# A windowed attention in front of two MoE layers: row-tiled transposes of the probabilities, and an output split taken from SBUF

## The chip, the core and the metric

The program runs on one core of one Trainium2 chip. The metric is the device time of one execution in microseconds (us). The kernel before has a median of 633.68 us over three runs (633.14 to 634.17).

## What is computed

Attention with a causal window of 128 keys and 4 sink keys over 2 batches of 8 heads, 768 positions, head size 64; then two dense layers (512 to 2048 to 512) over the 1536 tokens. All inputs are float64 or float32 on the host and are worked on as pairs of a high and a low part where precision asks for it.

```python
scores = scale * np.matmul(q, k.transpose(0, 1, 3, 2))
keep = is_sink | in_window                    # 4 sinks, window of 128
scores = np.where(keep, scores, -1000000000.0)
a = np.exp(scores - np.max(scores, axis=-1, keepdims=True))
a = a / (np.sum(a, axis=-1, keepdims=True) + 1e-09)
attn = np.matmul(a, v)
x = attn.transpose(0, 2, 1, 3).reshape(B * S, H * D)
h = np.maximum(x @ w_in, 0.0);  x = h * h @ w_out        # layer 1
h = x @ w_in2;  out = (h * np.tanh(softplus(h))) @ w_out2 # layer 2
```

## The kernel before

The attention takes the first 106 us and the two layers the rest. It goes over 12 tiles of 128 queries (batch b, block i of 6), and in each over 4 pairs of heads (j). One pass of the loop `for n in range(-3, NPR + 4)` (line 541) is called a step here; two steps, an even and an odd n, are a double step, and two double steps make a tile. A step works on several pairs at once, each at another stage, and the program writes the order of each engine's work out by hand:

- `emit_s` (line 350) makes the scores of pair n+4 on TensorE: for each of the two heads three matmuls over 64 rows (L356, high and low parts), into two PSUM banks `s` out of four.
- `emit_max` (L367, DVE) masks a head's scores in PSUM and takes the extreme into `nm`; `emit_exp` (L379, ACT) takes the exponential of pair n+3 into `pr` in SBUF, with its sum. The `s` banks of a pair are free when its exponentials are done, so the scores of pair n+6 wait for them.
- On even steps `emit_rs` (L390, L391, DVE) takes the reciprocals of two pairs' sums and `emit_norm` (L399, POOL) scales those pairs' probabilities, one pair per instruction. `emit_sink` (L440, POOL) gathers the sink columns of a tile's eight heads.
- On even steps `prep` transposes a block of k or q (`tr`, L302, four 128x128 transposes) for two tiles on; ACT takes the high part (L314) and DVE the low (L320).
- Also on even steps `emit_t` (line 401) transposes the probabilities of two pairs into `pt`, one PSUM bank for each pair: per head one 128x128 block, or two from the second block of a batch on (L407, L408). `evac_t` (L415) copies one pair's bank to `pts` in SBUF in each step, on DVE for the pair j = 0 and on ACT for the other three.
- On odd steps `emit_av` (L428) multiplies `pts` with v for two pairs into the one bank `av`; its column tiles are 64 wide. Once per tile, from the third block of a batch on, the sink columns are transposed (L449, `trs`), copied (L455, DVE) and multiplied (L464).
- When a tile is complete, `emit_x` and `split_x` take its output out of PSUM: ACT casts `av` to the high part `xh` (L477) and DVE subtracts that from `av` for the low part `xl` (L483). Both read the PSUM bank `av`, which the next tile's L428 needs.

```python
401  def emit_t(b, i, j):
403      pt = ps_p.tile([P, 2, 2, P], F32, tag="pt", name="pt")
407              nc.tensor.transpose(pt[:, 0, e, :], pr[b, i][:, h, op : op + P], ident)
408          nc.tensor.transpose(pt[:, 1, e, :], pr[b, i][:, h, oc : oc + P], ident)
474  def emit_x(b, i):
477      nc.scalar.copy(hi, x)
483      nc.vector.tensor_tensor(out=lo, in0=x, in1=f32(hi), op=ALU.subtract)
```

The scores, the transposes and the products with v use TensorE in three shapes: 64 rows by 128 columns (the two heads side by side in row halves), 128 by 128, and 128 rows by 64 columns (two heads in column halves). While the attention runs, `CONV_STEPS` places the conversion of the first four weight blocks of layer 1 between the steps (L131 and L166 on POOL, L137, L141 and L147 on DVE, L162 on ACT). Its last steps have no more scores; there the first matmuls of layer 1 (L620, `h`) stand between the rest of the attention on TensorE.

Of the kernel before, what the change touches and what calls it, by code (L numbers as in the profile page):

```python
# [9 lines left out]
F32 = mybir.dt.float32  # L10
# [18 lines left out]
def kernel(  # L29
# [314 lines left out]
    def sum_at(b, i, j):  # L344
        g, s = divmod(pair_no[b, i, j] + 1, 2)
        return sums[g % len(sums)], s
# [54 lines left out]
    def emit_t(b, i, j):  # L401
        _, _, _, op, oc, _ = geom(i)
        pt = ps_p.tile([P, 2, 2, P], F32, tag="pt", name="pt")
        for e in range(2):
            h = 2 * j + e
            if op is not None:
                nc.tensor.transpose(pt[:, 0, e, :], pr[b, i][:, h, op : op + P], ident)  # L407
            nc.tensor.transpose(pt[:, 1, e, :], pr[b, i][:, h, oc : oc + P], ident)  # L408
        st["pt", b, i, j] = pt

    def evac_t(b, i, j):
        pt = st.pop(("pt", b, i, j))
        pts = apool.tile([P, 2, 2, P], F32, tag="pts", name="pts", bufs=3)
        c = slice(0 if i else 1, 2)
        (nc.vector.tensor_copy if j in EV else nc.scalar.copy)(pts[:, c], pt[:, c])  # L415
        st["pts", b, i, j] = pts
# [3 lines left out]
    def emit_av(b, i, j):  # L420
# [3 lines left out]
        pts = st.pop(("pts", b, i, j))  # L424
# [18 lines left out]
    def emit_sink_t(b, i, free):  # L443
# [4 lines left out]
        pt = free[0][:, 512 - P :] if free else ps_p.tile([P, P], F32, tag="pt", name="trs")  # L448
# [25 lines left out]
    def emit_x(b, i):  # L474
        hi, lo = x_slot(b, i)
        x = av.pop((b, i))
        nc.scalar.copy(hi, x)  # L477
        st["x"] = (x, hi, lo)
# [15 lines left out]
    with tc.manual_schedule():  # L494
# [46 lines left out]
        for n in range(-3, NPR + 4):  # L541
            at = {d: pairs[n + d] for d in range(-3, 5) if 0 <= n + d < NPR}
# [14 lines left out]
            if -3 in last:  # L557
                emit_x(*at[-3][:2])
            if 4 in at and n > -3:
                emit_max(*at[4], 0)  # L560
                emit_max(*at[4], 1)
            split_x()


            if n % 2 == 0:
                if n >= 0:
                    prep(t + 2, "kq"[j // 2])
                for d in (-1, 0):
                    if d in at:
                        emit_t(*at[d])  # L570
                if -1 in last:
# [454 lines left out]
```

## Time and profile before

| | |
|---|---|
| median of three runs | 633.68 us |
| the profiled execution, its own time | 634.14 us |
| its span (first to last instruction) | 632.4 us |
| TensorE busy (PE) | 624.2 us, 99% |
| VectorE busy (DVE) | 461.9 us, 73% |
| ScalarE busy (ACT) | 363.7 us, 58% |
| GpSimd busy (POOL) | 71.1 us, 11%, all of it in the attention |
| granted TensorE clock | full in all 40 slices of the span |

The shares of the last column are means over stages that differ: the attention uses all engines, the layers mostly TensorE. PE's busy time is that of matmuls with modelled ends that overlap; the distance between the starts of two matmuls says what one costs in a row. PEld is the loading of the stationary operand, which overlaps the matmul before it.

### The profile page before, as it was taken

To read this page: it belongs to the slowest core of one execution; us is meant where nothing else is said; L and a number is where in the kernel's file an instruction comes from. 1 tells how busy PE (TensorE), PEld (TensorE's weight loads), DVE (VectorE), ACT (ScalarE), POOL (GpSimd) and SP (SyncE) were. 2 spreads that over 40 slices of the span, in tenths; PEclk is the share of its full clock that TensorE was granted. 3 is DMA by queue.
4 is the path that set the end of the run, shared out by engine and by line. 5 is a ranking of instruction groups with operands and counts; after the bars stand their busy time and mean duration, and the time that the engine had idled before them with its cause. 6 is when DMAs were issued, how large, how long until landed. Compare 5 with 4: busy or idle time off the path is not lost.

```text
span 632.4 us, 9265 instructions
## 1 busy us (share of the span) xinstructions
PE 624.2 (99%) x3382; PEld 515.9 (82%) x3382; DVE 461.9 (73%) x968; ACT 363.7 (58%) x745; POOL 71.1 (11%) x97
## 2 busy tenths in 40 slices
PE   8999999999999999999999999999999999999996
PEld 7778787888888888888888888888888888888885
DVE  5988983999852011138889869999888888888884
ACT  5988985777744333347777745555454444544442
POOL 4686773000000000000000000000000000000000
PEclk9999999999999999999999999999999999999999
DMA  8644630666630000005666600000010000010001
GB/s 200 148 118 104 164 120 26 195 204 201 199 101 1 2 0 1 0 1 169 197 199 199 192 10 1 0 2 1 1 66 1 1 1 1 1 67 0 2 0 69
DMA packets 61189, 46.83 MB, mean 74 GB/s; under 512 B 38996, under 2 KB 55636, under 8 KB 61140
## 3 DMA queue, kind: packets, MB, share of 16 engines
q1 hardware_dynamic: 60848, 45.82, 25.0%
q8 instruction: 27, 0.44, 0.3%
q10 hardware_dynamic: 292, 0.39, 0.2%
q14 instruction: 22, 0.18, 0.1%
HBM read 43.06 MB, written 3.15 MB: 73 GB/s over the span
## 4 chain that ended last, share of the span: by engine, by line
PE 96%; DVE 2%; ACT 1%; issue 0%; DVEq 0%
PE h L620 41%; PE o L636 41%; PE s L356 4%; PE av L428 3%; PE tr L302 2%; PE pt L408 1%; PE pt L407 1%; PE idle L517 1%; PE av L464 1%; DVE s L367 1%; ACT pr L379 0%; DVE cv_a L147 0%; DVE cv_r L137 0%; ACT kh L314 0%; DVE cv_r L141 0%
## 5 line engine op out<-in xcount | busy, mean ns | idle before, releaser
L620 PE MATMUL h<-xl,wih 128*128 128x512 f32 x384 | 103.2, 390 | 0.0
L620 PE MATMUL h<-xh,wil 128*128 128x512 f32 x384 | 103.0, 390 | 0.0
L620 PE MATMUL h<-xh,wih 128*128 128x512 f32 x384 | 102.6, 389 | 0.0
L694 DVE TENSOR_TENSOR gl<-h,gh 128x512 fp32r<-128x512 f32 x48 | 33.2, 691 | 93.0 <-ACT gh L690 92.9
L620 PEld LDWEIGHTS h<-xl,wih 128*128 128x128 f32 x384 | 72.0, 188 | 15.2 <-issue 0.3
L620 PEld LDWEIGHTS h<-xh,wih 128*128 128x128 f32 x384 | 72.1, 188 | 15.0
L620 PEld LDWEIGHTS h<-xh,wil 128*128 128x128 f32 x384 | 71.9, 188 | 15.0 <-issue 0.2
L710 ACT ACTIVATE e<-t,small 128x512 f32<-128x512 f32 x48 | 34.8, 726 | 70.1 <-DVE t L706 70.1
L636 PE MATMUL o<-gh,wol 128*128 128x512 f32 x192 | 74.7, 389 | 0.0
L636 PE MATMUL o<-gl,woh 128*128 128x512 f32 x192 | 74.7, 389 | 0.0
L636 PE MATMUL o<-gh,woh 128*128 128x512 f32 x192 | 74.7, 389 | 0.0
L688 ACT ACTIVATE h<-h 128x512 f32<-128x512 f32 x48 | 27.9, 582 | 77.5 <-PE h L620 77.4
L636 PE MATMUL o<-wol,gh 128*128 128x512 f32 x176 | 68.5, 389 | 0.0
L636 PE MATMUL o<-woh,gl 128*128 128x512 f32 x176 | 68.5, 389 | 0.0
L636 PE MATMUL o<-woh,gh 128*128 128x512 f32 x176 | 68.5, 389 | 0.0
L726 ACT CAST gh<-t 128x512 fp32r<-128x512 f32 x44 | 27.4, 623 | 46.6 <-PE o L636 42.9
L399 POOL TENSOR_TENSOR pr<-pr,rs 128x544 f32<-128x544 f32 (+2 forms) x48 | 48.4, 1022 | 23.4 <-DVE rs L391 13.3
L147 DVE SCALAR_TENSOR_TENSOR cv_a<-cv_a,cv_r 128x512 int32<-128x512 int32 x64 | 44.4, 694 | 6.1
L379 ACT ACTIVATE pr<-s,nm 128x272 f32<-128x272 f32 (+2 forms) x96 | 44.4, 476 | 5.0 <-DVE nm L367 2.6
L731 DVE TENSOR_TENSOR gl<-t,gh 128x512 fp32r<-128x512 f32 x44 | 30.3, 690 | 19.8 <-ACT gh L726 19.8
L636 PEld LDWEIGHTS o<-gh,wol 128*128 128x128 f32 x192 | 36.1, 188 | 7.5
L636 PEld LDWEIGHTS o<-gl,woh 128*128 128x128 f32 x192 | 36.0, 188 | 7.5
(121 smaller groups left out, 1101.2 us busy)
## 6 DMA issues: line engine op xcount, KB each, us to landing
raw<-in_moe_w_in_dram SPq DMA_DIRECT2D x32, 512.0 KB, 3.8
raw<-in_moe_w_out_dram SPq DMA_DIRECT2D x32, 512.0 KB, 4.0
vn<-in_v_dram SPq DMA_DIRECT2D x12, 256.0 KB, 3.0
kn<-in_k_dram SPq DMA_DIRECT2D x11, 256.0 KB, 3.7
qn<-in_q_dram SPq DMA_DIRECT2D x10, 256.0 KB, 4.1
out_dram<-ob SPq DMA_DIRECT2D x8, 256.0 KB, 2.2
qn<-in_q_dram SPq DMA_DIRECT2D x4, 128.0 KB, 3.0
out_dram<-o SPq DMA_DIRECT2D x2, 256.0 KB, 2.9
```

The costliest lines, as they stand in the source:

```text
L147: nc.vector.scalar_tensor_tensor(out=ai, in0=ai, scalar=3, in1=self.r, op0=ALU.logical_shift_left, op1=ALU.bitwise_or)
L356: nc.tensor.matmul(banks[e][:, 0:w], lhsT=x[b, i][r, j, :], rhs=y[r, j, c0 : c0 + w], start=(m == 0), stop=(m == 2),)
L379: nc.scalar.activation(out=pr[b, i][:, 2 * j + e, 0:w], in_=banks[e][:, 0:w], func=AF.Exp, bias=nm[:, e : e + 1], scale=-1.0, accum_out=sm ...
L399: nc.gpsimd.tensor_tensor(out=x, in0=x, in1=rs.to_broadcast([P, 2, w]), op=ALU.mult)
L428: nc.tensor.matmul(av[b, i][e * D : (e + 1) * D, j, :], lhsT=vn[b, kb][:, 2 * j + e, :], rhs=pts[:, c, e, :], start=(j == 0 and m == 0), s ...
L620: nc.tensor.matmul(ph, lhsT=w[a][:, d, :], rhs=x[:, d, :], start=(m == 0 and d == 0), stop=(m == 2 and d == NDC - 1),)
L636: nc.tensor.matmul(acc[sp][t], lhsT=a, rhs=x, start=(fb == 0 and m == 0), stop=(fb == NFB - 1 and m == 2),)
L688: nc.scalar.activation(out=ph, in_=ph, func=AF.Relu)
L694: nc.vector.tensor_tensor(out=gl, in0=hp.pop(n), in1=f32(gh), op=ALU.subtract)
L710: nc.scalar.activation(out=e, in_=t, func=AF.Ln, bias=two)
L726: nc.scalar.copy(g_tiles(n)[0], et[n][1])
L731: nc.vector.tensor_tensor(out=gl, in0=t, in1=f32(gh), op=ALU.subtract)
```

## The change

The transposes of the probabilities are done in two row halves, one for queries 0 to 63 and one for 64 to 127. A half has 64 rows, a stationary operand of 64 rows by 128 columns, and 64 moving columns of the identity; it writes 64 columns of the transposed block, and the two halves write different PSUM banks. So `emit_t` takes a group of two pairs, makes 16 half transposes in the place of 8 whole ones, and runs on odd steps, one step later than before, right behind that step's scores. The two banks are copied out in this step and the next (`evac_t`), the second of them on DVE for one group in two. Product, sink product and output follow one step later each; the loop has one step more. The reciprocals and the scaling are made for pairs n+2 and n+3 in place of n+1 and n+2. The sink transposition moves between the scores and the half transposes, its copy (`evac_sink`) between the two masks of the pair whose bank it uses. `emit_x` copies `av` to a float32 tile `xf` in SBUF on ACT, POOL casts that to the high part, and DVE's subtraction, one step later, reads `xf` and the high part from SBUF.

```diff
-        g, s = divmod(pair_no[b, i, j] + 1, 2)
+        g, s = divmod(pair_no[b, i, j], 2)
...
-    def emit_t(b, i, j):
...
+    def emit_t(group):
+        banks = [ps_p.tile([P, 2, 2, 2, P // 2], F32, tag="pt", name="pt") for _ in range(2)]
+        for s, (b, i, j) in enumerate(group):
+            _, _, _, op, oc, _ = geom(i)
+            for e in range(2):
+                for c, o in enumerate((op, oc)):
+                    if o is None:
+                        continue
+                    for r in range(2):
+                        rows = slice(r * D, (r + 1) * D)
+                        nc.tensor.transpose(
+                            banks[r][:, s, c, e, :], pr[b, i][rows, 2 * j + e, o : o + P], ident[rows, rows]
+                        )
+        pts = apool.tile([P, 2, 2, 2, P], F32, tag="pts", name="pts", bufs=2)
+        for s, p in enumerate(group):
+            st["pts", p] = pts[:, s]
+        st["evac"] = [(group, banks[r], pts[..., r * D : (r + 1) * D], r) for r in range(2)]
...
+        group, x, y, r = st["evac"].pop(0)
+        copy = nc.vector.tensor_copy if r and pair_no[group[0]] % 4 in EV else nc.scalar.copy
...
     def emit_x(b, i):
         hi, lo = x_slot(b, i)
-        x = av.pop((b, i))
-        nc.scalar.copy(hi, x)
+        x = apool.tile([P, NPAIR, P], F32, tag="xf", name="xf", bufs=1)
+        nc.scalar.copy(x, av.pop((b, i)))
+        nc.gpsimd.tensor_copy(hi, x)
         st["x"] = (x, hi, lo)
...
+            if 0 in last:
+                emit_sink_t(*at[0][:2], st["s", *at[4]][0][1] if 4 in at else None)
...
+            if 4 in at and n > -3:
+                emit_max(*at[4], 0)
+            evac_sink()
+            if 4 in at and n > -3:
+                emit_max(*at[4], 1)
             if n % 2 == 0:
-                group = [at[d] for d in (1, 2) if d in at]
+                group = [at[d] for d in (2, 3) if d in at]
...
-            if -3 in last:
-                emit_x(*at[-3][:2])
...
             split_x()
...
+            if -4 in last:
+                emit_x(*at[-4][:2])
...
+            if n % 2:
+                if 0 in at:
+                    emit_t([at[-1], at[0]])
+            else:
                 if n >= 0:
                     prep(t + 2, "kq"[j // 2])
...
-                for d in (-3, -2):
+                for d in (-4, -3):
                     if d in at:
                         emit_av(*at[d])
```

On TensorE, in a tile with sinks, the program before has the end of an even step, the odd step behind it and the next scores as follows (`s` scores, `pt` transposes of probabilities, L449 the sink's, `av` the products, L464 the sink's).

```order
L407 MATMUL pt<-ident,pr 128x128
L408 MATMUL pt<-ident,pr 128x128
L449 MATMUL s<-ident,psg 128x128
L356 MATMUL s<-kh,qh 128x272 x2
L356 MATMUL s<-kh,ql 128x272 x2
L356 MATMUL s<-kl,qh 128x272 x2
L428 MATMUL av<-pts,vn 64x128 x8
L464 MATMUL av<-pst,vs 64x128 x8
L356 MATMUL s<-kh,qh 128x272 x2
```

Before it in the same even step stand the scores, the four `tr` and the other transposes. The program after the change has, from an odd step's scores to the end of the even step behind it:

```order
L356 MATMUL s<-kh,qh 128x272 x2
L356 MATMUL s<-kh,ql 128x272 x2
L356 MATMUL s<-kl,qh 128x272 x2
L462 MATMUL s<-ident,psg 128x128
L411 MATMUL pt<-ident,pr 128x64 x16
L356 MATMUL s<-kh,qh 128x272 x2
L356 MATMUL s<-kh,ql 128x272 x2
L356 MATMUL s<-kl,qh 128x272 x2
L302 MATMUL tr<-ident,kn 128x128 x4
L441 MATMUL av<-pts,vn 64x128 x8
```

The 8 transposes of 128 columns became 16 of 64 between two runs of scores, which use the same 64 rows by 128 columns; `tr` and `av` now follow each other; the sink's transposition (L462) alone stands between scores and half transposes, once per tile.

On DVE, the same tile before: two masks, the reciprocals, two masks of the next step's pair, the split of a finished output (L483) and the low part of q (L320).

```order
L390 TENSOR_REDUCE rs<-sum_103 128x4 [waits Activation_49,Pool_49]
L391 RECIPROCAL rs<-rs 128x4 [waits DVE_49]
L367 ISA s,nm<-s,mask_o 128x272 [waits PE_49]
L367 ISA nm 128x1
L367 ISA s,nm<-s,mask_o 128x272 [waits PE_49]
L367 ISA nm 128x1
L483 TENSOR_TENSOR xl_70<-av,xh_67 128x4x128 [waits Activation_49]
L320 TENSOR_TENSOR ql<-tr,qh 128x512 [waits Activation_49]
```

The split waits for ACT's cast there. After the change:

```order
L367 ISA s,nm<-s,mask_e 128x272 [waits PE_49,Activation_49]
L367 ISA nm 128x1
L390 TENSOR_REDUCE rs<-sum_104 128x4 [waits Activation_49]
L391 RECIPROCAL rs<-rs 128x4 [waits DVE_49]
L497 TENSOR_TENSOR xl_70<-xf,xh_67 128x4x128 [waits Pool_49]
L320 TENSOR_TENSOR kl<-tr,kh 128x4x128 [waits Activation_49]
```

The split now stands right behind the reciprocals, with both masks ahead of them, and waits for POOL.

On POOL, before, the scalings of two pairs follow each other, with the sink columns or a weight block between them:

```order
L399 TENSOR_TENSOR pr<-pr,rs 128x544
L131 TENSOR_SCALAR cv_a<-raw 128x512
L399 TENSOR_TENSOR pr<-pr,rs 128x544 x3
L440 COPY psg<-pr 128x128
```

After the change the cast of a finished output stands between the scalings of two groups:

```order
L453 COPY psg<-pr 128x128
L131 TENSOR_SCALAR cv_a<-raw 128x512
L399 TENSOR_TENSOR pr<-pr,rs 128x544 x2
L491 CAST xh_69<-xf 128x4x128
L399 TENSOR_TENSOR pr<-pr,rs 128x544 x2
```

The cast is POOL's one new instruction, twelve times in the program, behind the scalings of the group before it.

## Rows read from the trace of the kernel before

**Rows 1.** Stretches (nine tiles, tail): length; busy PE, PEld, DVE, ACT, POOL; clock; DMA.

```profile
18.11:25.29 7.18, 7.14 (x74) 5.66 (x72) 6.74 (x28) 7.13 (x25) 5.99 (x7) 1.00 0.74 186
25.29:32.53 7.24, 7.24 (x82) 5.97 (x80) 6.51 (x27) 7.00 (x23) 4.75 (x6) 1.00 0.41 93
32.53:41.84 9.31, 8.31 (x99) 7.00 (x97) 8.44 (x27) 7.25 (x24) 6.92 (x8) 1.00 0.58 153
41.84:50.08 8.24, 8.24 (x100) 6.97 (x98) 6.88 (x28) 7.34 (x23) 7.51 (x8) 1.00 0.44 100
50.08:57.95 7.87, 7.87 (x99) 6.91 (x97) 6.59 (x26) 6.51 (x23) 5.31 (x9) 1.00 0.45 103
57.95:65.14 7.19, 7.13 (x85) 5.88 (x83) 5.76 (x24) 6.22 (x21) 4.22 (x7) 1.00 0.38 107
65.14:72.21 7.07, 7.07 (x74) 5.66 (x72) 6.57 (x25) 6.94 (x25) 5.77 (x6) 1.00 0.84 191
72.21:79.82 7.61, 7.61 (x82) 6.18 (x81) 7.52 (x29) 6.86 (x22) 4.45 (x5) 1.00 0.40 115
79.82:88.38 8.56, 8.56 (x99) 7.14 (x97) 7.02 (x28) 7.48 (x25) 7.41 (x8) 1.00 0.32 116
88.38:106.22 17.84, 17.42 (x199) 13.71 (x197) 9.95 (x37) 10.98 (x32) 10.13 (x10) 1.00 0.20 62
```

**Rows 2.** Busy time of nearly all of the two layers after the attention, same columns.

```profile
155.00:632.00 477.00, 472.40 (x2085) 390.95 (x2083) 335.31 (x561) 242.18 (x409) 0.00 (x0) 1.00 0.16 50
```

**Rows 3.** Timeline of PE, one double step: start, length, engine, line, operands.

```profile
75.83 0.70 PE L356 MATMUL s<-kh,qh 64*128 64x272 f32 x2
...
76.71 0.66 PE L302 MATMUL tr<-ident,qn 128*128 128x128 f32 x4
77.20 0.27 PE L407 MATMUL pt<-ident,pr 128*128 128x128 f32 x1
...
78.17 0.39 PE L356 MATMUL s<-kh,qh 64*128 64x272 f32 x2
78.40 0.28 PE L356 MATMUL s<-kh,ql 64*128 64x272 f32 x2
78.53 0.29 PE L356 MATMUL s<-kl,qh 64*128 64x272 f32 x2
78.80 1.09 PE L428 MATMUL av<-pts,vn 128*64 128x128 f32 x16
79.82 0.39 PE L356 MATMUL s<-kh,qh 64*128 64x272 f32 x1
```

**Rows 4.** Timeline of PE, transposes right behind a change of shape.

```profile
93.36 0.33 PE L407 MATMUL pt<-ident,pr 128*128 128x128 f32 x1
93.53 0.27 PE L408 MATMUL pt<-ident,pr 128*128 128x128 f32 x1
93.64 0.27 PE L407 MATMUL pt<-ident,pr 128*128 128x128 f32 x1
```

**Rows 5.** Groups of weight loads on PEld: busy us, mean ns, idle before and releaser.

```profile
L428 PEld LDWEIGHTS av<-pts,vn 128*64 128x64 f32 x352 | 18.8, 136 | 5.9 <-PE s L356 2.0 <-issue 1.7 <-DVE xl L483 0.4
L408 PEld LDWEIGHTS pt<-ident,pr 128*128 128x128 f32 x94 | 12.9, 141 | 0.0
L356 PEld LDWEIGHTS s<-kh,qh 64*128 64x128 f32 x84 | 9.0, 183 | 8.4 <-issue 3.4 <-ACT pr L379 2.5 <-ACT qh L314 1.2
```

**Rows 6.** POOL: line L399 (min/median/max ns), and the sink copy's group.

```profile
L399 POOL TENSOR_TENSOR pr<-pr,rs x48: 612/1092/1542, 11.6 to 99.8; 128x544 f32<-128x544 f32 x32, 128x256 f32<-128x256 f32 x8, 128x512 f32<-128x512 f32 x8
...
L440 POOL COPY psg<-pr 128x128 f32<-128x128 f32 x8 | 2.3, 290 | 0.5
L131 POOL TENSOR_SCALAR cv_a<-raw 128x512 f32<-128x512 f32 x4 | 6.1, 1534 | 0.0
```

**Rows 7.** Timeline of DVE and POOL where a two-input DVE instruction meets two scalings.

```profile
89.75 2.59 POOL L399 TENSOR_TENSOR pr<-pr,rs 128x544 f32<-128x544 f32 x2 [2.42 <-DVE rs L391]
90.64 0.76 DVE L147 SCALAR_TENSOR_TENSOR cv_a<-cv_a,cv_r 128x512 int32<-128x512 int32 x1
```

More of the change, by code (lines that the diff above doesn't have):

```diff
@@ L399, in emit_norm, with evac_t @@
         nc.gpsimd.tensor_tensor(out=x, in0=x, in1=rs.to_broadcast([P, 2, w]), op=ALU.mult)
-    def emit_t(b, i, j):
[L402 to L416, printed above, removed]
+    def emit_t(group):
[15 more added lines that the diff above has]
+        st["evac"] = [(group, banks[r], pts[..., r * D : (r + 1) * D], r) for r in range(2)]
+    def evac_t(eng=None):
+        if not st.get("evac"):
+            return
+        group, x, y, r = st["evac"].pop(0)
+        copy = nc.vector.tensor_copy if r and pair_no[group[0]] % 4 in EV else nc.scalar.copy
+        c0 = [0 if i else 1 for _, i, _ in group]
+        if len(set(c0)) == 1:
+            copy(y[:, : len(group), c0[0] :], x[:, : len(group), c0[0] :])
+        else:
+            for s, c in enumerate(c0):
+                copy(y[:, s, c:], x[:, s, c:])
     av = {}
@@ L423, in emit_av @@
             av[b, i] = ps_a.tile([P, NPAIR, P], F32, tag="av", name="av")
-        pts = st.pop(("pts", b, i, j))
+        pts = st.pop(("pts", (b, i, j)))
         blocks = [(1, i)] if op is None else [(0, i - 1), (1, i)]
@@ L446, in emit_sink_t @@
         g = st.pop("sink")
-        pt = free[0][:, 512 - P :] if free else ps_p.tile([P, P], F32, tag="pt", name="trs")
+        pt = free[:, 512 - P :] if free is not None else ps_p.tile([P, P], F32, tag="pt", name="trs")
         nc.tensor.transpose(pt, g.rearrange("p h s -> p (h s)"), ident)
@@ L540 @@
         emit_exp(*pairs[0])
-        for n in range(-3, NPR + 4):
-            at = {d: pairs[n + d] for d in range(-3, 5) if 0 <= n + d < NPR}
+        for n in range(-3, NPR + 5):
+            at = {d: pairs[n + d] for d in range(-4, 5) if 0 <= n + d < NPR}
             last = {d for d in at if at[d][2] == NPAIR - 1}
@@ L556 @@
                         emit_sink(*p[:2])
-            if -3 in last:
-                emit_x(*at[-3][:2])
-            if 4 in at and n > -3:
-                emit_max(*at[4], 0)
-                emit_max(*at[4], 1)
-            split_x()
-            if n % 2 == 0:
+            split_x()
+            if -4 in last:
[3 more added lines that the diff above has]
+                    emit_t([at[-1], at[0]])
+            else:
                 if n >= 0:
                     prep(t + 2, "kq"[j // 2])
[L568 to L571, printed above, removed]
-                    emit_sink_t(*at[-1][:2], st["s", *at[4]][0] if 4 in at else None)
-            else:
-                for d in (-3, -2):
+                for d in (-4, -3):
                     if d in at:
                         emit_av(*at[d])
-                if -2 in last:
-                    emit_sink_mm(*at[-2][:2])
-            if -1 in at:
-                evac_t(*at[-1])
+                if -3 in last:
+                    emit_sink_mm(*at[-3][:2])
+            evac_t()
             if n in (-3, -2):
@@ L583 @@
             place_prep()
-            evac_sink()
             if n >= 0 and j == NPAIR - 1:
```

## The prediction

> **What bounds the kernel now.** I read the busy time by stretch first, then one double step on TensorE, then the lengths of what the change touches. In the two layers TensorE never runs dry: 2085 matmuls in 477 us, 0.229 us each [rows 2]. Nothing there is touched, so whatever time the attention loses or gains is lost or gained by the whole. In the attention TensorE is busy through nearly every one of nine tiles, 70.27 us together, and in the tail [rows 1]. But the reader should see how close the others stand: ACT fills 7.13 of 7.18 us in the first stretch, 7.00 of 7.24 in the second, 6.94 of 7.07 in the seventh, and DVE 7.52 of 7.61 in the eighth. Only the other five stretches, 7.19 to 9.31 us, have a TensorE that is longer than its neighbours by more than a few tenths. So a lighter TensorE gains there, and elsewhere meets ACT or DVE at once.
>
> **TensorE, a double step.** From 75.83 to 79.82 one takes 3.99 us [rows 3]. Its first scores take 0.88, the second, without a wait, 0.63; the 0.25 is a wait. Without it the sum is 0.63 (scores) + 0.49 (four `tr`, 76.71 to 77.20) + 0.97 (eight `pt`, 77.20 to 78.17) + 0.63 + 1.02 (`av`, 78.80 to 79.82) = 3.74 us. Whole transposes start 0.11 apart, and the first of a run is followed after 0.17 [rows 4]: 0.06 is a weight load or a matmul that nothing covers. Eight at 0.11 are 0.88, so going from one shape to another costs 0.09 more. Scores show the same: 0.23, then 0.13 [rows 3].
>
> The change takes the transposes into the scores' shape. I write X for two half transposes, one in each row half. An odd step is then 0.23 + 0.13 + 0.12 = 0.48 for the scores, with no change of shape behind them, and 8X. The even step's scores come without a change ahead: 3 x 0.12 + 0.09 = 0.45. Four `tr` with a change behind them are 0.58, `av` stays at 1.02. The sum is 2.53 + 8X.
>
> X is what no row shows. Scores run their two row halves side by side: the matmuls come as pairs (x2) with one distance for both [rows 3]. A half has half of the moving columns but the same 128 columns to load. If the matmul sets the 0.11, X is 0.055; if the load does, 0.11, and so it is, too, if the halves don't overlap. The loads decide it: a `pt` load takes 141 ns, like the 136 of a 64-column load of `av` and unlike the 183 of a 128-column load of the scores [rows 5]. So the load is the short one, the 0.06, and X is near the low end. I take 0.06: 3.01 us, 0.73 less than 3.74. At 0.11 it is 3.41, 0.33 less.
>
> The sink's transposition cost 0.11 among its like. Alone between scores and half transposes it costs a change each way and an uncovered load: 0.11 + 2 x 0.09 + 2 x 0.06 = 0.41. A tile with sinks saves 2 x 0.73 - 0.30 = 1.16 us on TensorE (0.36 at X = 0.11).
>
> **ACT and DVE.** Their work stays: as many exponentials, masks and copies of 512 columns; one copy of `av` has a new target, and one subtraction new sources. I cost both at no difference. So I put the larger of DVE, ACT and the lighter TensorE into each stretch [rows 1]: 7.13, 7.00, 8.44 (DVE), 7.34, 6.7 (7.87 - 1.16), 6.4 (7.19 - 0.8, a tile of small blocks), 6.94, 7.52, 7.48. The sum is 64.95. In the four stretches where ACT or DVE nearly fills the time, it fills 99, 97, 98 and 99%; I divide by 0.98: 66.3 us. Gain: 70.27 - 66.3 = 4.0 us.
>
> **Tail.** From 88.38 to 106.22 ACT and DVE have 11 and 10 us of 17.84 [rows 1], and don't limit. Two double steps with scores save 1.46, two later groups 16 x 0.05 = 0.8; two sink transpositions cost 0.6. Four matmuls of layer 1 stand among the rest in place of six, so two run afterwards, 0.46 [rows 2]. That is 1.2 less; the chain of the last pairs (scale, transpose, copy, multiply) is one step longer with less work to cover it, so I count 0.8.
>
> **POOL and the new wait.** The cast of an output to its high part comes to POOL: 512 columns, four times the sink copy's 128 at 0.29, so 1.16; the nearest upper row is 1.53 for a weight block of 512 columns [rows 6]. POOL's nine stretches sum to 52.3 us [rows 1]; 9 x 1.16 more make 62.8 in 66.3, so POOL keeps up, with little air. It is queued behind two scalings of 1.09, in front of two others. The scalings have a step more of slack than before, and their transposes should not wait. The split on DVE does: it waits for the cast where it waited for ACT, and behind it stand the low part of k, a copy and the next masks, for which ACT's exponentials and then the score banks wait. From one set of reciprocals to the split behind the next is a double step, some 3.5 us; two scalings and the cast take 3.34. That just fits, except where a weight block's 1.53 comes first, in about one tile of three. A wait of 1.4 less DVE's air of some 0.5 in a tile, three times, is 2.7 at most; none is the other end, if POOL has caught up by then. I take 1.0. What is won beside it, that `av` is free after one copy, is in the stretches already.
>
> The Trainium skill ("SBUF — State Buffer", section "Who interferes with whom") says that a DVE instruction with two SBUF inputs contends with a GpSimd instruction that reads SBUF, and that whoever comes first holds the port for all of its instruction. The trace agrees in one place: two scalings beside a two-input DVE instruction took 2.59 us in the place of 2 x 1.09, and it 0.76 [rows 7]. By that rule the twelve splits, which now read SBUF alone, could each hold or be held for up to 1.09, 13 us in all at the worst; my sum has 1.0.
>
> **Sum.** 4.0 + 0.8 - 1.0 = 3.8 us. The profiled execution took 634.14 (632.4 of span and 1.7 around it), 0.46 over the median; it would take 630.3, and the median goes from 633.68 to **629.9 us**.
>
> **Rivals.** *The halves gain nothing* (X = 0.11). Then only changes of shape are saved, 0.36 per tile with sinks. The stretches of 8.24, 7.87 and 8.56 lose that each, the one of 9.31 0.7 of its waits, the rest 0.3 together: 2.1. The tail saves 0.66 and pays 1.06, and half a microsecond goes to the split: 1.2 less, 632.5. The equal spacing of all loads and matmuls speaks for it, the loads' lengths against it.
>
> The Trainium skill ("TensorE: Matmul & The Clock Gate", section "Wait — 56ns, not 53.3ns?") gives some 62 ns per MATMUL as an issue cost when the sequencer decodes it. By that, 16 half transposes take 0.99 us, X = 0.124, and 633.3 would come out. The trace speaks against it: 16 `av` matmuls, with a change of shape and an uncovered load, took 1.02, so 0.054 each [rows 3].
>
> *ACT and DVE give it back.* The reciprocals now wait for exponentials of the same step, and even steps on DVE (two masks, reciprocals, split or copy, low part) are over twice the odd ones. If the two score banks per pair can't level that, each tile keeps its length and only waits change owner: 633.3. The four stretches that ACT and DVE fill to 97 to 99% speak against it.
>
> *Slower: the split waits for POOL in every tile.* The margin above is 0.2 us. If the cast is late by a weight block's length or by a port's, DVE waits 1.4 in each tile. DVE's own nine stretches sum to 62.0, 6.89 each; 8.29 with the wait makes 74.6, 4.3 more than now, less 0.8 in the tail: 637.2. It decides from a wait of 1.0 per tile on; below that the time stays under the old one. For it: POOL's 62.8 of 66.3. Against it: only a third of the tiles have a block in front.
>
> **Numbers.** My forecast has 70%: with its own bounds (no loss to POOL, no 2%, tail of 1.2: 6.5, and X = 0.055 some tenths; or POOL's 2.7) it goes from 626.9 to 631.8. Halves without gain, by load or issue: 10%. Given back: 10%. Slower by POOL: 8%. That the halves run one after the other at 0.11 each, 0.22 a pair, which would be slower too: 2%. Up to 633.8 the range takes in the second and third and leaves out the slower. 0.2% is 1.3 us, about what a measurement can tell. Faster by more: the 70 and half of the first rival, 0.75. Within: the other half and the given-back case, 0.15. Slower: the last two, 0.10.
>
> **What would show it.** Half transposes in pairs some 0.06 apart, scores behind them without the 0.09, no stretch of a tile over 8.7 us, ACT at 95% or more of most stretches. L497's idle time on DVE, released by POOL, under 2 us in all; over 9 us, the slower rival holds. Whole pairs 0.11 apart: the first rival. If the scores' idle time released by ACT or DVE grows by as much as the transposes shrink, it was given back. The time of the layers must stay; if it moves, I have the wrong place altogether.

## The result, and the profile after

The change takes 638.99 us (median of 6 runs, 636.7 to 640.21), the kernel before, on the same chip, 633.41 (6 runs, 633.04 to 634.17). The ratio is 1.0074, with a 95% interval of 1.0063 to 1.0085: slower by 5.6 us. The prediction, 629.9 with a range of 626.9 to 633.8, was wrong, in sign and in range.

The profiled execution took 639.14 (637.4 of span), 5.0 more than that of before. First its time by stretches, which answers to [rows 1]: the nine tiles and the tail, bounded as there by the first scores of a tile, same columns (length; busy PE, PEld, DVE, ACT, POOL; clock; DMA).

```profile
18.01:24.54 6.53, 6.32 (x86) 4.82 (x84) 6.02 (x25) 6.29 (x24) 5.61 (x7) 1.00 0.92 229
24.54:31.85 7.31, 7.24 (x105) 5.64 (x102) 6.82 (x27) 7.01 (x23) 6.22 (x8) 1.00 0.03 7
31.85:41.89 10.04, 8.52 (x121) 6.73 (x117) 9.01 (x27) 6.96 (x22) 7.96 (x9) 1.00 0.59 151
41.89:50.60 8.71, 8.34 (x123) 6.61 (x118) 7.07 (x28) 7.41 (x23) 8.21 (x10) 1.00 0.41 94
50.60:58.36 7.76, 7.63 (x121) 6.39 (x117) 6.92 (x25) 6.37 (x22) 6.00 (x8) 1.00 0.45 103
58.36:65.77 7.41, 7.33 (x104) 5.92 (x100) 6.28 (x27) 6.90 (x23) 4.67 (x9) 1.00 0.39 89
65.77:73.35 7.58, 6.50 (x87) 4.77 (x84) 7.12 (x25) 6.20 (x23) 7.30 (x7) 1.00 0.99 238
73.35:83.47 10.12, 9.20 (x106) 6.92 (x101) 8.81 (x30) 7.89 (x24) 7.72 (x10) 0.83 0.16 36
83.47:91.64 8.17, 8.09 (x119) 6.47 (x117) 6.67 (x25) 7.46 (x23) 6.96 (x7) 1.00 0.62 212
91.64:110.69 19.05, 16.72 (x247) 13.21 (x241) 12.05 (x37) 10.67 (x31) 11.91 (x13) 1.00 0.18 57
```

The nine stretches take 73.63 us, 3.4 more than before's 70.27; the tail 19.05, 1.2 more than 17.84. The rest, some 0.5, fits the matmuls of layer 1 that stood in the tail and now run behind it. The layers themselves did not move; this row answers to [rows 2]:

```profile
160.00:637.00 477.00, 472.34 (x2084) 390.76 (x2082) 335.29 (x561) 242.17 (x409) 0.00 (x0) 1.00 0.16 50
```

The reader should see two things in the table. Seven stretches are within 0.7 us of before, some shorter, some longer, where four of them were forecast to shrink by 0.8 to 1.2. And two stand out: 10.04 in place of 9.31, and 10.12 in place of 7.61, the latter with a mean clock of 0.83.

**The halves as such.** Timeline of PE in the last tile, which answers to [rows 3] (start, length, engine, line, operands):

```profile
83.46 0.37 PE L356 MATMUL s<-kh,qh 64*128 64x272 f32 x2
...
84.01 0.66 PE L302 MATMUL tr<-ident,kn 128*128 128x128 f32 x4
84.60 1.09 PE L441 MATMUL av<-pts,vn 128*64 128x128 f32 x16
85.62 0.39 PE L356 MATMUL s<-kh,qh 64*128 64x272 f32 x2
...
86.11 0.83 PE L411 MATMUL pt<-ident,pr 64*128 64x64 f32 x15
86.77 0.39 PE L356 MATMUL s<-kh,qh 64*128 64x272 f32 x1
...
87.24 0.39 PE L356 MATMUL s<-kh,qh 64*128 64x272 f32 x1
...
91.12 0.71 PE L411 MATMUL pt<-ident,pr 64*128 64x64 f32 x16
91.64 0.37 PE L356 MATMUL s<-kh,qh 64*128 64x272 f32 x2
```

Where nothing waits, 16 half transposes take 0.52 us from the first to the scores behind them (91.12 to 91.64). That is 0.065 a pair; the prediction took 0.06. Eight whole ones took 0.97 [rows 3]. The 62 ns a MATMUL that the Trainium skill ("TensorE: Matmul & The Clock Gate", section "Wait — 56ns, not 53.3ns?") gives with hardware decode off are not seen here: 0.033 each. So the new operation is as cheap as hoped. But right behind the halves of the odd step the first score bank's matmul starts at 86.77 and the second bank's at 87.24. On PEld the reason stands beside its load (idle before it, and who ended it):

```profile
87.24 0.18 PEld L356 LDWEIGHTS s<-kh,qh 64*128 64x128 f32 x1 [0.29 <-ACT pr L379]
```

It waits for the exponential that frees the bank. In the list of waits (engine, line, waited for: us in total, times, longest) of the first 130 us of the change, and behind it of the kernel before:

```profile
PEld s L356 <- ACT pr L379: 8.0, 25, 1.2
```

```profile
PEld s L356 <- ACT pr L379: 2.8, 13, 0.6
```

**The long tile from 31.85.** Timeline of POOL, DVE, ACT and PE:

```profile
30.31 2.14 POOL L399 TENSOR_TENSOR pr<-pr,rs 128x544 f32<-128x544 f32 x2 [0.54 <-ACT qh L314]
...
32.43 1.54 POOL L131 TENSOR_SCALAR cv_a<-raw 128x512 f32<-128x512 f32 x1
...
33.92 0.62 POOL L491 CAST xh<-xf 128x512 fp32r<-128x512 f32 x1
...
34.50 2.60 POOL L399 TENSOR_TENSOR pr<-pr,rs 128x544 f32<-128x544 f32 x2
34.57 1.57 DVE L497 TENSOR_TENSOR xl<-xf,xh 128x512 fp32r<-128x512 f32 x1 [0.50 <-POOL xh L491]
...
36.07 0.68 DVE L320 TENSOR_TENSOR kl<-tr,kh 128x512 fp32r<-128x512 f32 x1
36.67 0.71 DVE L137 TENSOR_SCALAR cv_r<-raw 128x512 int32<-128x512 int32 x1
...
36.81 0.66 PE L302 MATMUL tr<-ident,qn 128*128 128x128 f32 x4 [0.53 <-DVE kl L320]
...
37.42 0.47 DVE L141 TENSOR_SCALAR cv_r<-raw 128x512 uint16<-128x512 uint32 x1
...
38.32 0.49 ACT L379 ACTIVATE pr<-s,nm 128x272 f32<-128x272 f32 x1 [2.26 <-DVE nm L367]
...
41.43 0.68 PE L411 MATMUL pt<-ident,pr 64*128 64x64 f32 x15 [0.91 <-DVE pts L426]
```

The cast stands behind two scalings and a weight block's 1.54. The split waits 0.50 for it, then takes 1.57 in place of its usual 0.66, and the two scalings beside it 2.60 in place of 2.14. Behind the split on DVE stand the low part of k, two instructions of the weight block (L137 and L141, some 1.1 together) and only then the next masks, so ACT has nothing to do for 2.26 us. TensorE itself stands still for 0.53 us, until the low part of k has been read out of `tr`, and later for 0.91, until a copy on DVE has freed a bank of the transposes. The Trainium skill ("SBUF — State Buffer", section "Who interferes with whom") has this case: a DVE instruction with two SBUF inputs contends with a GpSimd instruction that reads SBUF, and the shared ports are an exclusive lock. The trace agrees: the split is 0.91 longer than usual, the two scalings together 0.46. Line L497 as a whole (min/median/max ns), and what DVE waited for ahead of it:

```profile
L497 DVE TENSOR_TENSOR xl<-xf,xh x12: 659/662/1575, 26.7 to 112.1; 128x512 fp32r<-128x512 f32 x12
its engine sat idle before it (us, times) until:
  POOL xh L491: 5.3, 4
```

Of these 5.3 us, 3.33 belong to the last output, at 112.10, whose cast waited for ACT's copy at the very end of the attention. The other three waits, 0.50, 0.39 and 1.11, are those of the three casts right behind a weight block.

**The long tile from 73.35.** Here TensorE's granted clock was 0.50, its lower level (1.2 of 2.4 GHz), in stretches that ran at 1.00 in the kernel before; before it fell, TensorE had been busy for only 6.50 of 7.58 us in the tile ahead. (The tile from 31.85, busy for 8.52 of 10.04, was not followed by a fall, so what decides it is not shown.) One such stretch (same columns as the first table), and the group of matmuls on PE that starts in it:

```profile
80.00:81.00 1.00, 1.00 (x11) 0.97 (x12) 0.96 (x6) 0.90 (x3) 0.67 (x2) 0.50 0.00 0
```

```profile
80.03 1.98 PE L441 MATMUL av<-pts,vn 128*64 128x128 f32 x16
```

The same 16 `av` matmuls take 1.09 in the timeline above. Two runs of the change with a mean clock of 0.999 took 636.7 and 637.35; the four with 0.995 or 0.996 took 638.83 to 640.21.

### The profile page after: what moved, and what is told of

Same layout as the page of the kernel before. It is cut to its first block, busy times and chain, and to the rows that moved or that the text cites. A ratio compares the mean times of both kernels' runs of the same rounds, so it can differ in the third digit from the quotient of the medians.

```text
span 637.4 us, 9633 instructions
## 1 busy us (share of the span) xinstructions
PE 623.4 (98%) x3558; PEld 512.4 (80%) x3558; DVE 466.7 (73%) x966; ACT 363.4 (57%) x745; POOL 81.9 (13%) x109
## 4 chain that ended last, share of the span: by engine, by line
PE 88%; DVE 5%; ACT 4%; POOL 2%; issue 1%; DVEq 0%; POOLq 0%; ACTq 0%
PE o L648 41%; PE h L632 41%; ACT pr L379 2%; PE s L356 2%; PE tr L302 1%; DVE s L367 1%; POOL pr L399 1%; PE av L441 1%; ACT pts L426 1%; PE idle L531 1%; PE pt L411 1%; DVE cv_a L147 1%; DVE xl L497 1%; DVE cv_r L137 0%; PE av L477 0%
## 5 line engine op out<-in xcount | busy, mean ns | idle before, releaser
L399 POOL TENSOR_TENSOR pr<-pr,rs 128x544 f32<-128x544 f32 (+2 forms) x48 | 51.6, 1096 | 21.7 <-DVE rs L391 16.3
L147 DVE SCALAR_TENSOR_TENSOR cv_a<-cv_a,cv_r 128x512 int32<-128x512 int32 x64 | 45.7, 715 | 6.1
```

What stands on the lines that cost most here:

```text
L147: nc.vector.scalar_tensor_tensor(out=ai, in0=ai, scalar=3, in1=self.r, op0=ALU.logical_shift_left, op1=ALU.bitwise_or)
L399: nc.gpsimd.tensor_tensor(out=x, in0=x, in1=rs.to_broadcast([P, 2, w]), op=ALU.mult)
```

## The experiments

All times are medians of 5 to 12 runs, beside runs of the kernel before on the same chip, which had medians between 633.3 and 633.7. Ratios are to those. Two of these kernels that lie less than some 1.5 us apart have intervals that overlap; such a difference is read as a hint, not as shown. The change's interval also touches, at its lower end, those of x_from_psum, split_two_later and change_blocks_odd, 2.2 to 3.3 us below it; the pair with whole transposes, 638.5 and 635.8, is clear of each other.

### Taking the change apart

**x_from_psum** is the change with the old output path (ScalarE casts from PSUM, VectorE subtracts from PSUM):

```
-        x = apool.tile([P, NPAIR, P], F32, tag="xf", name="xf", bufs=1)
-        nc.scalar.copy(x, av.pop((b, i)))
-        nc.gpsimd.tensor_copy(hi, x)
+        x = av.pop((b, i))
+        nc.scalar.copy(hi, x)
...
-            split_x()
             if -4 in last:
                 emit_x(*at[-4][:2])
+            split_x()
```

> The change with its output path undone: ACT casts the high part out of PSUM and DVE subtracts from PSUM, both in the step in which the copy stood; the half transposes and the new order stay. If the split through POOL and SBUF is what costs (its waits for the cast, and the port it shares with POOL's scalings), the time falls from 639.0 to 632 or less, and the split takes 0.69 us in every tile. If the new order of the steps costs (reciprocals behind the exponentials of the same step, even steps that are too heavy on DVE), it stays at 636 to 639.

635.73 us, ratio 1.0048 [1.0032, 1.0065]. **before_new_split** is the kernel before with the new output path alone (copy to `xf`, cast on GpSimd, split one step later):

> The kernel before with the new output path alone: copy to SBUF on ACT, cast on POOL, subtraction from SBUF one step later; whole transposes, old order. If the split costs by itself, 636 to 638 against 633.4, with splits of 1.5 us beside scalings. If it costs only where TensorE has been made lighter, 633 to 634, since here the split has an odd step to itself.

637.63, ratio 1.0063 [1.005, 1.0076]. **whole_transposes** is the change with whole 128-column transposes in the places of the halves, one bank for a pair:

```
-                    for r in range(2):
-                        rows = slice(r * D, (r + 1) * D)
-                        nc.tensor.transpose(
-                            banks[r][:, s, c, e, :], pr[b, i][rows, 2 * j + e, o : o + P], ident[rows, rows]
-                        )
+                    nc.tensor.transpose(banks[s][:, c, e, :], pr[b, i][:, 2 * j + e, o : o + P], ident)
```

> The change with whole 128-column transposes at the same places in the order, in the place of the row halves; all else as changed. If TensorE no longer bounds the tiles, 638 to 641, since only TensorE's slack goes. If it still does, the halves' 0.4 us per double step and the saved changes of shape are lost again, some 22 times 0.55: 647 to 651.

638.51, ratio 1.0081 [1.0068, 1.0094]. **order_only** is x_from_psum with the same whole transposes, so that the new order (with its later steps and moved copies) is left:

> The change with both its edits undone and its order kept: output path from PSUM as before, whole transposes, but one step later, with the new places of reciprocals, sink copy and copies. If the new order is harmless and the row halves lower the clock, it comes out at 633 to 634 with the full clock, below the 635.7 of the run with the halves. If the order costs by itself, 635 to 636 with the full clock.

635.83, ratio 1.0039 [1.0026, 1.0053]. The four corners (639.0 and 638.5 with the new split, 635.7 and 635.8 without) say what follows: the new split costs 3.3 us in the new order with halves, 2.7 with whole transposes, and 4.2 in the old order. The halves bring 0.1 or lose 0.5, which is nothing by the intervals. But not at the same clock: all six runs of x_from_psum had a mean clock of 0.993 to 0.997, eight of the ten of order_only 1.000. In the profiled executions the nine stretches less the eighth take 61.09 us with halves and 62.85 with whole transposes, so 1.8 less; the eighth gives back 1.2 of that, 10.77 at a mean clock of 0.84 against 9.60 at the full one.

The new order costs 2.4 by itself, and most of it lies in that eighth stretch. The nine of order_only take 72.45 us, 2.2 more than before's 70.27; the eighth alone 9.60 against 7.61, 2.0 more. This row answers to the eighth of [rows 1], and behind it stands order_only's timeline of POOL, DVE and PE:

```profile
72.38:81.98 9.60, 7.75 (x83) 6.09 (x82) 8.92 (x31) 7.62 (x24) 5.50 (x7) 1.00 0.13 31
```

```profile
71.34 2.32 POOL L399 TENSOR_TENSOR pr<-pr,rs 128x544 f32<-128x544 f32 x2
...
72.74 1.23 DVE L141 TENSOR_SCALAR cv_r<-raw 128x512 uint16<-128x512 uint32 x1
...
75.46 1.09 PE L433 MATMUL av<-pts,vn 128*64 128x128 f32 x16 [1.85 <-DVE xl L488]
```

The kernel before, in the same tile:

```profile
72.24 0.47 DVE L141 TENSOR_SCALAR cv_r<-raw 128x512 uint16<-128x512 uint32 x1
```

In the new order the weight block's L141 meets two scalings and takes 1.23 in place of 0.47. The masks stand behind it on DVE, the split (L488) behind those, and `av` waits for the split; TensorE stands still for 1.85 us (2.52 in x_from_psum). This is read from the profiles; no run tests it alone. The fifth change of tile shape (with whole transposes a double step has five in place of four) does make quiet tiles longer, 8.54 where before has 8.24 [rows 1] (row below, in the last test); but with other tiles shorter, the nine stretches less the eighth come out only 0.2 longer together (62.85 against 62.66).

### What the split loses

Stretch by stretch in the profiled executions, change against x_from_psum: six of the nine are within some 0.2 us. The two whose splits took 1.57 and 1.51 us, right behind a weight block, are 1.35 and 1.07 longer (10.04 against 8.69, 7.58 against 6.51); the eighth is 0.65 shorter, since `av` does not wait for the split there. The tail, up to its last sink product, takes 18.07 against 16.18. So the loss is not one of every tile.

**split_two_later**: the subtraction waits for the next odd step (`if n % 2 or n == NPR + 4: split_x()`).

> The change with DVE's split moved by one more step, into an odd step, where DVE has only two masks; cast and port as in the change. If the wait for the cast and the crowded even step cost, 634 to 636. If the port costs (the split locks out a scaling or is locked out), the split still shows 1.5 us or the scalings 1.45, and the time stays at 637 to 639.

636.83, ratio 1.0056 [1.0043, 1.0069]: 2.2 less than the change. A later split does not escape the scalings:

```profile
L497 DVE TENSOR_TENSOR xl<-xf,xh x12: 660/1066/1612, 27.7 to 110.0; 128x512 fp32r<-128x512 f32 x12
```

With before's path (x_from_psum) the same line, one of whose inputs is in PSUM, has no such spread; but `av` has to wait for it, and this wait is what the new path does remove:

```profile
L496 DVE TENSOR_TENSOR xl<-av,xh x12: 681/686/691, 24.9 to 107.5; 128x512 fp32r<-128x512 f32 x12
...
  PE av L441: 6.1, 7
```

**cast_on_scalar**: the change with `nc.scalar.copy(hi, x)` in place of `nc.gpsimd.tensor_copy(hi, x)`.

> The change, with the cast of the output's high part on ScalarE instead of GpSimd, out of the same SBUF copy; the subtraction on VectorE stays as in the change. Theory that the split's loss is both GpSimd's queue (5.3 us of waits in the profile) and VectorE's two-SBUF-operand subtraction beside GpSimd's scalings: the waits for GpSimd vanish, single subtractions still take up to 1.5 us, time 636.5 to 638. Rival A, the queue alone: 635.5 to 636.5, as x_from_psum. Rival B, the contention alone: 638.5 to 640.

637.59, ratio 1.0061 [1.0048, 1.0074]. By the medians, taking the cast out of GpSimd's queue takes off 1.4 of the 3.3 (the intervals overlap, so this is a hint). The longest split is 1156 ns now, in place of 1575. What stays, 1.9, is the contention together with ScalarE's extra cast of 0.59 a tile; this run does not part them.

**blocks_odd_steps** and **change_blocks_odd** move the weight blocks' steps on VectorE to odd steps, in x_from_psum and in the change:

```
-    CONV_AT = (5, 9)
-    CONV_STEPS = {0: "load", 5: "head_pool", 7: "mid_r", 8: "mid_or", 11: "high", 12: "low_pool"}
+    CONV_AT = (6, 8)
+    CONV_STEPS = {0: "load", 5: "head_pool", 7: "mid_r", 11: "mid_or", 13: "high", 14: "low_pool"}
```

> The run with the output from PSUM and the half transposes, with the weight blocks' three DVE instructions moved to the odd steps in which DVE has least (one block every 8 steps in the place of 9). If the wait of 5.4 us per pair near 71 us and the lower clock behind it come from DVE being locked there by POOL in a crowded step, both go: 630 to 632, clock 0.999. If TensorE's lighter load lowers the clock anyway, or the order costs, it stays at 635 to 636.

> The change as it is, with the same move of the weight blocks' steps. If the output path costs by meeting the weight blocks (cast queued behind a block on POOL, DVE's split and block in one step), 633 to 635. If it costs in every tile, through the port that split and scalings share, 636 to 637.

638.42 [1.0056, 1.0085] and 636.55 [1.0036, 1.0065]. The change gains 2.4, and its splits take 659 to 693 ns, so where the blocks fall seems a good part of its loss; the expectation had given 636 to 637 to the port in every tile, but the splits no longer show it. x_from_psum loses 2.7, all six runs with a mean clock of 0.991 to 0.996, a miss by either expectation.

### Where the halves' gain went

**halves_doubled**: x_from_psum with every half transpose made twice (`for r in (0, 1, 0, 1)`).

> The run with the output from PSUM and the half transposes, with every half transpose made twice into the same place: 0.5 us more of TensorE per double step, some 11 us in all. If odd steps have that much slack (the scores of the next step wait for ACT's exponentials anyway), and the busier TensorE keeps its clock, the time stays at 635 to 637, with the full clock. If TensorE bounds odd steps, 644 to 647.

639.89, ratio 1.0092 [1.0079, 1.0106]. A tile with two double steps has 32 more halves, 1.04 us at 0.52 for 16. Its last tile grew by 0.36, from 8.38 to 8.74 (stretch below, all of it busy on PE). So in this tile two thirds of the added work fell into time that TensorE had to spare in x_from_psum. It is one of the best: the nine stretches less the eighth grew by 4.5 us together for 7.8 of added work (one of them has only 16 more halves), so somewhat under half was free.

```profile
83.49:92.23 8.74, 8.74 (x153) 7.35 (x149) 7.26 (x28) 7.76 (x24) 7.83 (x8) 1.00 0.55 193
```

Two runs tried to fill that spare time by another order. **q_prep_odd** and **all_prep_odd** move the transposes of the next tile's q, or of q and k, from the even to the odd step of x_from_psum (the edit of all_prep_odd):

```
                     emit_t([at[-1], at[0]])
-            else:
                 if n >= 0:
                     prep(t + 2, "kq"[j // 2])
+            else:
```

> The same run with the transposes of q moved from the even step that also has the products and the sink's products to the odd step before it, behind the half transposes. If the gain of the halves is lost because steps have become uneven (0.9 to 1.3 us odd, 2.1 to 3.5 even on TensorE, with the scores only two pairs ahead), evening them out wins: 631 to 634. If not, 635 to 637, as without.

> The same with the transposes of k, too, in the other odd step: one more change of shape per double step than in the run without (0.15), but both kinds of step near 1.65 us on TensorE. By the theory of uneven steps 631 to 634; ACT has up to 2.8 us in one odd step then, which may take 1 to 2 of it back. By the rival 636 to 638.

640.17 [1.007, 1.0117] and 653.31 [1.0293, 1.0337]: misses. The steps became more even and other waits came up; in all_prep_odd the scores wait for q itself (9.1 us for its high part, 8.2 for its low, from 18 to 115 us), and the mean clock was 0.980 to 0.987.

**copy_swapped** and **change_copy_swapped** leave the order and swap which engine makes which of two copies (`not r` for `r` in the choice of VectorE), in x_from_psum and in the change:

> Before's output path with the new order and the half transposes; of the two output-bank copies in a row tile's double step, VectorE takes the one in the odd step and ScalarE the one in the even step (in x_from_psum it is the other way round). Theory that the halves' gain is held by single steps (the exponential behind ScalarE's copy releases the score bank late in the odd step, while ScalarE is idle in the even one): the even step of 3.52 us shortens toward 3.0, a tile of 8.25 toward 7.7, and the time is 632 to 634; 634 to 635 where the TensorE clock still falls for single windows. Rival (the steps are bound by something else, or the copy only moves the wait to VectorE's scalings): 635 to 637, as x_from_psum with 635.7.

> The change as it stands, with the same two copies swapped between VectorE and ScalarE. Theory of the uneven steps: 636 to 637, about 2 to 3 below the change's 639.0, since the split's waits for GpSimd stay. Rival: 638.5 to 640, no difference.

636.05 [1.0023, 1.0047] and 638.58 [1.0067, 1.0093]: no difference, a miss again. The long step of the tile with sinks stays at 3.52 us; moving ScalarE's work within the double step does not help.

**halves_old_order** and **halves_old_order_late** put the halves alone into the order of before (`emit_t([at[-2], at[-1]])` behind the transposes of k or q in the even step). In the first both banks are copied in that step; in the second the output products come two steps later.

> The kernel before with the half transposes alone: its own output path and its own order (transposes of a double step right behind the next tile's k or q in the even step, as before, so four changes of shape), only that the two pairs of one double step are taken together, the first pair one double step later, and that both banks are copied in the even step. Theory that the new order eats the halves' gain (it makes a fifth change of shape and packs TensorE's work into one of two steps): the gain shows here, tiles 0.3 to 0.4 shorter than before's, 630 to 632. Rival (the pairs are held by ScalarE and VectorE and the score banks whatever TensorE does, or the clock falls): 633 to 635. If the output product waits for the second copy, above 635.

> As halves_old_order, with the output products, the sink's product and the output path two steps later, so that the second bank's copy has a step of its own (as in the kernel before) and no product waits for it. Theory: 631 to 633, the drain at the end being two steps longer (about 1). Rival: 634 to 636.

637.53 [1.0052, 1.0079] and 637.15 [1.0031, 1.0062]. In the first the output product waits for the copies: from 18 to 108 us its weight loads wait 13.3 us for ACT's.

In the second it does not, but the clock falls. Its two runs with a mean clock of 0.997 and 0.998 took 634.65 and 635.02, the other five 637.0 to 639.3. In the profiled one TensorE was busy for only 1.01 of 2.00 us and then ran at 0.50:

```profile
74.00:76.00 2.00, 1.01 (x8) 0.56 (x6) 2.00 (x7) 1.01 (x5) 1.47 (x2) 0.99 0.75 168
76.00:78.00 2.00, 1.87 (x21) 1.58 (x21) 1.97 (x8) 1.85 (x5) 1.07 (x2) 0.50 0.00 0
```

So the new order does not seem to be what hides the halves: in the old one, with a clock near full and a drain that is two steps longer, they do not beat before's 633.6 either.

**The test that decided.** If the exponentials on ScalarE hold the score banks once TensorE is lighter, a lighter ScalarE must bring the halves' gain out, and must bring nothing where TensorE still is the bound. Three runs leave out the sums that the exponentials gather, and with them eight reads of ScalarE's accumulator in each row tile; the scalings use a constant:

```
-                bias=nm[:, e : e + 1], scale=-1.0, accum_out=sm[:, s, e, 0:1],
+                bias=nm[:, e : e + 1], scale=-1.0,
...
-            nc.vector.memset(x, 1e-9)
+            nc.vector.memset(x, 0.5)
```

> x_from_psum (new order, half transposes, before's output path) without the sums that the exponentials gather: the eight reads of ScalarE's accumulator of each row tile are left out (0.21 to 0.27 us each, some 1.8 us of ScalarE's 7.0 a tile), and the scalings use a constant. Theory that after the halves ScalarE's loop (score banks wait for the exponential) holds the pairs, not TensorE: with ScalarE lighter the halves' 3.7 us come out, 630 to 632, and 3 to 4 us below order_only_no_sums. Rival (the pairs are held elsewhere: VectorE, GpSimd, or the clock): within 1 us of order_only_no_sums.

> order_only (new order, whole transposes, before's output path) with the same sums left out. Theory: TensorE is the bound here, so it gains little from a lighter ScalarE, 634 to 636 (order_only 635.8). Rival (ScalarE held it too): 631 to 633.

> The kernel before with the same sums left out. Theory (TensorE bounds the tiles of before): 632 to 633.5, next to no gain. Rival (ScalarE holds the pairs of before as well): 628 to 631.

632.67 (ratio 0.9977 [0.9962, 0.9991]), 636.22 (1.0035 [1.0022, 1.0048]) and 633.55 (0.9997 [0.9989, 1.0006]). With whole transposes, in either order, a lighter ScalarE brings nothing: 636.2 against 635.8, 633.55 against 633.7. With halves it brings 3.1 us, and the halves are now worth 3.55 in place of 0.1. The last tile of each shows the same: order_only, order_only_no_sums, x_from_psum, x_from_psum_no_sums, before_no_sums, columns as in the first table.

```profile
81.98:90.52 8.54, 8.54 (x99) 6.93 (x98) 6.70 (x26) 7.21 (x23) 7.66 (x8) 1.00 0.61 198
```

```profile
82.62:91.16 8.54, 8.54 (x98) 6.92 (x97) 6.70 (x26) 6.48 (x15) 7.63 (x8) 1.00 0.59 199
```

```profile
81.18:89.56 8.38, 8.15 (x122) 6.67 (x117) 6.99 (x28) 7.36 (x25) 7.80 (x8) 1.00 0.67 216
```

```profile
76.04:83.86 7.82, 7.63 (x120) 6.34 (x117) 6.62 (x27) 6.54 (x15) 7.31 (x8) 1.00 0.69 234
```

```profile
79.71:87.94 8.23, 8.23 (x99) 6.96 (x97) 6.76 (x28) 6.75 (x16) 7.33 (x8) 1.00 0.32 115
```

With whole transposes TensorE is busy for all of the tile and the length does not change with ScalarE's load (8.54 and 8.54). With halves it changes: 8.38 to 7.82. Yet ScalarE was busy for only 7.36 of the 8.38. An engine can set the pace without being full, because the banks let scores run only two pairs ahead. The other tiles say the same, whatever the clock did: the nine stretches less the eighth take 62.85 us with whole transposes and 62.81 without sums as well; with halves they take 61.09 with sums (x_from_psum) and 58.42 without (x_from_psum_no_sums):

```profile
sum 61.09, PE 58.32 PEld 47.02 DVE 54.56 ACT 54.60 POOL 48.10; mean PE 7.29 PEld 5.88 DVE 6.82 ACT 6.83 POOL 6.01
```

```profile
sum 58.42, PE 55.54 PEld 45.70 DVE 53.26 ACT 49.03 POOL 47.03; mean PE 6.94 PEld 5.71 DVE 6.66 ACT 6.13 POOL 5.88
```

The edit does one thing more: the reciprocals no longer wait for the exponentials. It does not tell ScalarE's time from that wait; both belong to the loop of exponentials and sums. x_from_psum_no_sums still has clock falls: five of its 12 runs, with a mean clock of 0.997 or more, took 629.7 to 631.2; the other seven, with 0.992 to 0.995, took 632.3 to 634.2.

## Why the prediction was wrong

**The price of a half pair: right.** 0.065 in place of 0.06, and scores follow the halves without the 0.09. The two rivals that rested on X, no gain by load or issue and halves one after the other, are out.

**TensorE's sum: mis-sized.** The step "3.01 us, 0.73 less than 3.74" is off at both ends. A double step of before without waits takes about 3.63 (the stretch of 8.24 [rows 1] is two of them and the sink's product, 0.97). One of the change takes 0.95 + 2.16 = 3.11: 0.95 is the odd step where nothing waits (x_from_psum), 2.16 the even one above (83.46 to 85.62). There the scores ahead of `tr` take 0.55, not 0.45; I had left out the change of shape behind them. So it saves 0.52. A tile with sinks needs 2 x 3.11 + 0.97 + 0.40 for the sink's transposition = 7.59, and saves 0.65 in place of 1.16. With that, and 0.57 for my 0.8 in the stretch of 7.19 (by 0.52 to 0.73), my own sum over the nine stretches (7.13, 7.00, 8.44, 7.59, 7.22, 6.62, 6.94, 7.52, 7.91, by 0.98) gives 67.7, a gain of 2.6 and not 4.0. Two slips of mine change nothing in it: in the stretch of 9.31 DVE (8.44) already stood above TensorE (8.31), and the 631.8 comes to 631.6 by its own terms.

**"ACT and DVE": the step that failed.** I put the largest engine's busy time into each stretch, divided by 0.98, and got 66.3 us; the nine stretches took 73.63, and 71.86 in x_from_psum, without the new split. That holds when engines can run ahead within a tile; here scores run two pairs ahead and no more. The change puts the odd step at 0.95 of TensorE and the even one at 2.16 or 3.13 (with the sink's product). ScalarE's exponentials come at their own pace, so the second bank of the even step comes free late. Tiles with sinks came out at 8.17 and 8.71 where before had 8.56 and 8.24. The runs without sums show that the exponentials with their sums are the holder, and that before was not held by them. "Their work stays" was wrong as well: the new order moved scalings against weight blocks, L141 on DVE went from 0.47 to 1.23 us in the eighth tile, and that tile has most of the 2.4 that the order costs. What does not follow from the runs is which order would let the halves out: the attempts by another order (q_prep_odd, all_prep_odd, halves_old_order, halves_old_order_late) failed, so this stays open. The rival *ACT and DVE give it back* was right in kind, and the four stretches at 97 to 99% that I held against it were no evidence: they show that an engine can be full, not that it must be full before it holds the others.

**"POOL and the new wait": mis-sized.** I took 1.0; the new path costs 3.3 (639.0 against 635.7). Two parts of the term were off in opposite directions. The cast takes 0.61, not 1.16, so POOL is not short of time: its nine stretches sum to 60.7 of 73.6. But the contention that I set aside, with my sum at 1.0, is there: a split of 1575 ns in place of 660, and two scalings of 2.60 in place of 2.14 beside it. L497's waits for POOL were 5.3 us; under 2 was to show me right, over 9 the slower rival. Without the last output's 3.33 they were 2.0: the waits ahead of it were small, and what the 1.0 did not count was the longer split behind two of them. The slower rival's mechanism, a weight block ahead of the cast, acts in three tiles of twelve and not in each.

**The tail: wrong sign.** 1.2 more in place of 0.8 less. In x_from_psum the tail behaves as forecast, 16.95 from 89.56 to the start of its last `av` matmul at 106.51, against 17.64 in before by the same marks; so what turned it round is the new output path.

**The clock: missing from the prediction.** In some executions it fell to half after TensorE had stood still, which took 2 to 3 us from a run; that was no term of my sum. What decides it is not shown: the standstill of 1.85 us in order_only was not followed by a fall.

Together, by the medians: 2.4 for the new order alone, 0.1 off for the halves, 3.3 for the new output path make the 5.6 (the 0.1 at unlike clocks, see above).

## What to carry to other kernels

Taking work from the bounding engine pays only up to the next holder, and that one is not found by comparing busy sums per tile: go step by step, ask how many buffers let the producer run ahead, and whose instruction frees them. A cheap test is to leave work out on the suspected holder, once in the old and once in the new kernel; only if the second moves alone has the bound passed over. And a copy out of PSUM that saves a wait can be paid for if the next instruction then has two SBUF inputs beside a busy GpSimd. A new order also decides which instructions run beside each other: one step of a weight block went from 0.47 to 1.23 us that way.

## What was not expected of the hardware

Half transposes of 64 rows overlap: 16 take 0.52 us, 0.033 each, and a pair 0.065 where a whole one takes 0.11 [rows 4]. GpSimd's cast of 128x512 took 0.61 us, 0.05 less than VectorE's subtraction of that size and far less than its own 1.53 for a weight block of that size. TensorE's clock fell in the middle of the attention: in x_from_psum PE stood still for 2 us, and the next stretches had mean clocks of 0.61 and 0.54.

```profile
72.00:74.00 2.00, 0.00 (x0) 0.00 (x0) 2.00 (x7) 0.90 (x4) 0.35 (x1) 1.00 0.00 1
74.00:76.00 2.00, 1.85 (x18) 1.55 (x20) 1.96 (x9) 1.99 (x8) 0.20 (x1) 0.61 0.03 8
76.00:78.00 2.00, 2.00 (x28) 2.00 (x28) 1.14 (x5) 0.36 (x3) 1.95 (x2) 0.54 0.00 0
```

In none of the three profiled executions with whole transposes in the order of before did it fall there, in one of the three with whole transposes in the new order, and with halves in ten of fourteen. So a change that lightens TensorE, or makes it stand still, can lose on the clock part of what it wins in matmuls.
